# State-space kernel and its parameter gradients: phases from three-piece bf16 matmuls wrapped by an integer mask, inner sums over 128 positions

## The chip, the core and the metric

The kernel runs on one core of one Trainium2 chip. The metric is the device time of one launch in microseconds (us); where several timed runs of a kernel are quoted, it is their median. PE is the matmul engine, VectorE (DVE in the profile), ScalarE (ACT) and GpSimd (POOL) are the other compute engines.

## The reference, cut to what matters

The block is a layernorm, a diagonal state-space convolution, a gated feed-forward network, and the gradients of all of it. The change touches what makes the convolution kernel and its parameter gradients:

```python
# D = 576 channels, N = 128 states, L = 2048 positions
logdA = dt * (A_re + 1j * A_im)
P = jnp.exp(logdA[:, :, None] * l[None, None, :])       # D x N x L
K = jnp.einsum("dn,dnl,dn->dl", Cc, P, dB).real         # the convolution kernel
y = irfft(rfft(pad(xn)) * rfft(pad(K)))[..., :L] + u * Dskip
out = x + y * silu(ffn(xn))
# wanted: out and the gradients of u, A, B, C, log_dt, Dskip, w1, w3, w2
```

The complex exponential is never formed for all L positions. A position is split as an inner and an outer part, l = inner + width x outer; exp, sine and cosine are made for the inner table (Q) and for the outer one (P), and products of the two are summed by matmuls over the states. The gradient of A, B, C and dt needs sums of gK(l) P(l) and of l gK(l) P(l) over all l, and uses the same split.

## The kernel before

It has three parts that matter here. **Kernel generation**: for each chunk of 16 channels, fp32 matmuls against selector matrices (constants with one run of numbers per channel) make phase and decay rate times position; VectorE reduces the phase to a fraction of a turn in two fp32 passes; ScalarE takes sine, absolute value and cosine.

```python
# kernel generation, one chunk (cut)
pt = ps.tile([P, 512], FP32, name="tau_ps")
nc.tensor.matmul(pt[:], lhsT=self.thp[rows, c, :], rhs=SELQ[rows, cols], ...)   # fp32
nc.scalar.copy(out=tauQ[:, j * 512:(j + 1) * 512], in_=pt[:])
pe = ps.tile([P, 512], FP32, name="e_ps")
nc.tensor.matmul(pe[:], lhsT=self.rho[rows, c, :], rhs=SELQ[rows, cols], ...)   # fp32
nc.scalar.activation(out=EQ[:, j * 512:(j + 1) * 512], in_=pe[:], func=ACT.Exp)
...
# gen_trig
nc.vector.tensor_scalar(out=u[:], in0=tau[:], scalar1=MAGIC, scalar2=-MAGIC, op0=ALU.add, op1=ALU.add)
nc.vector.tensor_tensor(out=fr[:], in0=tau[:], in1=u[:], op=ALU.subtract)
nc.scalar.activation(out=S[:], in_=fr[:], func=ACT.Sin, scale=TWO_PI_S)
nc.scalar.activation(out=A[:], in_=fr[:], func=ACT.Abs)
nc.scalar.activation(out=C[:], in_=A[:], func=ACT.Sin, scale=-TWO_PI_S, bias=self.halfpi_col[:])
```

**The correlation gradient gK**: PE's inverse transform, written in halves of 64 positions; ScalarE stores it as `gK2[:, :, jpos]`, bf16 elements 64 bytes apart.

```python
for h in range(2):
    ...
    nc.tensor.matmul(pt[64 * h:64 * (h + 1), 0:DH], lhsT=lw, rhs=rh, ...)     # 64 output rows
nc.scalar.copy(out=gK2[:, :, jpos], in_=pt[:, 0:DH])
```

**The parameter sums**: a loop over 36 pieces; VectorE multiplies rates broadcast to 64 rows by the position, reduces them, forms Q; PE contracts Q with gK over 64 positions; ScalarE copies the result out of PSUM; VectorE makes four long fp32 passes and one reduction.

```python
nc.vector.tensor_tensor(out=prodR[:], in0=Tsb[:], in1=Pzr[:, :, None, :].to_broadcast(...), op=ALU.mult)
nc.vector.tensor_tensor(out=prodI[:], in0=Tsb[:], in1=Pzi[:, :, None, :].to_broadcast(...), op=ALU.mult)
nc.vector.tensor_tensor(out=comb[:, :, 0:2, :], in0=prodR[:, :, 0:2, :], in1=prodI[:, :, 2:4, :], op=ALU.subtract)
nc.vector.tensor_tensor(out=comb[:, :, 2:4, :], in0=prodR[:, :, 2:4, :], in1=prodI[:, :, 0:2, :], op=ALU.add)
nc.vector.reduce_sum(out=red[:]..., in_=comb[:]..., axis=AX.X)
```

## Time and profile before

The kernel before took 3373.16 us (median of three runs, 3367.8 to 3374.43). The page of the profile gives the busy time of each engine over the span, and then the span in 40 slices with the busy share in tenths:

```profile
span 3370.4 us, 46694 instructions
...
PE 2351.0 (70%) x19198; PEld 1532.3 (45%) x19198; DVE 1926.4 (57%) x2713; ACT 1468.8 (44%) x1878; POOL 263.5 (8%) x503
...
PE   1999994845999794836231111129999999965999
PEld 1444442532333572625121111117777777753777
DVE  6677778475444457365889999954334443310222
```

One slice is 84 us. PE is full in slices 2 to 6 (kernel generation), VectorE in slices 22 to 26 (the parameter sums), so the averages of 70% and 57% hide two stages that each have a bound of their own. Each stage ends with its last VectorE work, except the convolution and feed-forward, which are cut where the first matmul of the gK stage starts:

| Stage of the kernel before | us | bound by |
|---|---|---|
| start, layernorm, kernel generation | 552.7 | PE, fp32 matmuls |
| convolution and feed-forward | 732.7 | not touched |
| gK and input gradient | 425.9 | PE and VectorE in turns |
| parameter sums | 486.7 | VectorE |
| final gradients, left behind the loop | 24.9 | VectorE, small instructions |
| feed-forward gradients to the end | 1147.5 | not touched |

These are two lines of VectorE's timeline before (start, length, instruction): passes that build the selectors stand between the layernorm's own short instructions.

```profile
22.74 4.41 DVE L297 SCALAR_TENSOR_TENSOR SELQ<-v 128x4096 f32<-128x4096 f32 x1
27.07 0.16 DVE L143 RECIPROCAL rstd<-sd 128x1 f32<-128x1 f32 x1
...
28.71 4.37 DVE L298 SCALAR_TENSOR_TENSOR SELQ<-v,SELQ 128x4096 f32<-128x4096 f32 x1
```

### The profile page before, as it was taken

The page shows a single profiled execution, that of the slowest core. Times are in us where ns is not written, and L with a number is a line of the kernel's source. Part 1 is how long each engine was busy: PE and PEld are TensorE (multiplying, and loading weights), DVE is VectorE, ACT ScalarE, POOL GpSimd, SP SyncE. Part 2 cuts the span into 40 slices and gives each one's busy share as a digit, 9 for nine tenths or more (in the row PEclk, how much of TensorE's full clock was granted, in tenths as well). Part 3 has the DMA queues.
Part 4 walks back from the last instruction along what each step waited for, and adds up shares of the span by engine and source line. Part 5 has one row for each costly group of instructions (what it writes and reads, how often), then busy time and mean ns, then how long its engine had stood idle before and what let it go on. Part 6 is the DMA issues. An engine that isn't in the chain of part 4 may idle for free.

```text
span 3370.4 us, 46694 instructions
## 1 busy us (share of the span) xinstructions
PE 2351.0 (70%) x19198; PEld 1532.3 (45%) x19198; DVE 1926.4 (57%) x2713; ACT 1468.8 (44%) x1878; POOL 263.5 (8%) x503
## 2 busy tenths in 40 slices
PE   1999994845999794836231111129999999965999
PEld 1444442532333572625121111117777777753777
DVE  6677778475444457365889999954334443310222
ACT  2888886601444113511055666527555555510000
POOL 1000000001111110000000000002222222110000
PEclk8555555977999896967665555559999999987999
DMA  2000000205666762011043333246544444347532
GB/s 79 19 21 21 22 21 13 101 34 183 236 225 218 251 208 97 1 41 51 27 124 97 100 96 96 69 132 172 148 136 140 137 138 137 108 103 203 201 148 82
DMA packets 323880, 373.57 MB, mean 111 GB/s; under 512 B 106577, under 2 KB 274898, under 8 KB 320466
## 3 DMA queue, kind: packets, MB, share of 16 engines
q1 hardware_dynamic: 172226, 132.36, 13.7%
q10 hardware_dynamic: 117888, 129.08, 12.3%
q0 software_dynamic: 33552, 109.15, 9.6%
q8 instruction: 150, 2.46, 0.3%
q14 instruction: 64, 0.52, 0.1%
HBM read 201.84 MB, written 152.14 MB: 105 GB/s over the span
## 4 chain that ended last, share of the span: by engine, by line
PE 40%; DVE 26%; issue 18%; DMA 7%; POOL 3%; SPq 3%; ACT 2%; ACTq 0%; POOLq 0%; DVEq 0%
PE px L1293 8%; PE ph L1200 4%; PE tau_ps L353 4%; PE e_ps L356 4%; PE dft_ps L496 3%; SPq L1105 3%; DVE red L1005 2%; PE gk_ps L857 2%; DVE prodI L997 2%; PE e_ps L365 2%; DMA out_dram<-gw 2%; PE pgw L1241 2%; PE tau_ps L362 2%; PE inv_ps L607 2%; PE pgw L1229 2%
## 5 line engine op out<-in xcount | busy, mean ns | idle before, releaser
L984 PE MATMUL pT<-gK,QTr 64*128 64x32 bf16 x576 | 71.0, 185 | 331.7 <-DVE QTr L970 318.7
L1293 PE MATMUL px<-w1T,ggc 128*128 128x288 bf16 x1152 | 237.8, 289 | 42.1 <-DMA w1T<-in_B_w_dram 42.1
L1293 PE MATMUL px<-w3T,guc 128*128 128x288 bf16 x1152 | 237.6, 289 | 27.5 <-DMA guc<-GU_dram 19.1
L1241 PEld LDWEIGHTS <-xn_bf 128*128 128x128 bf16 x2304 | 226.7, 99 | 58.5 <-issue 29.9
L984 PEld LDWEIGHTS <-QTr 64*128 64x128 bf16 x1152 | 64.5, 101 | 355.0 <-DVE QTr L970 322.5
L691 DVE CAST g_t<-pg 128x1024 bf16<-128x1024 f32 x72 | 88.2, 1224 | 182.3 <-ACT s_t L690 182.3
L1244 DVE CAST gw<-pgw 128x256 bf16<-128x256 f32 x144 | 60.1, 423 | 228.1 <-DMA out_dram<-gw 130.7
L683 PEld LDWEIGHTS <-wmB_w 128*128 128x128 bf16 x1152 | 107.4, 98 | 161.6 <-issue 44.2
L1297 DVE TENSOR_TENSOR gx<-px,gx 128x288 f32<-128x288 f32 x32 | 13.1, 452 | 291.4 <-PE px L1293 291.4
L1200 PE MATMUL ph<-go_oT,w2T 128*128 128x512 bf16 x720 | 169.6, 382 | 0.5 <-ACT gh L1203 0.5
L1310 ACT ACTIVATE t<-gx 128x576 f32<-128x576 f32 x16 | 10.9, 683 | 362.1 <-DVE gx L1297 362.1
L1229 PE MATMUL pgw<-go_o,h_n 128*128 128x288 bf16 x1152 | 165.4, 286 | 0.0
L727 PE MATMUL po<-w2res,hc 128*128 128x288 bf16 x1152 | 146.4, 289 | 17.4 <-DMA hc<-H_dram 17.4
L1241 PE MATMUL pgw<-gg_n,xn_bf 128*128 128x256 bf16 x1152 | 135.0, 279 | 26.7 <-DVE gw L1244 26.7
L690 ACT ACTIVATE s_t<-pg 128x1024 bf16<-128x1024 f32 x72 | 73.8, 1024 | 168.7 <-PE pu L688 168.7
L1293 PEld LDWEIGHTS <-ggc 128*128 128x128 bf16 x1152 | 113.6, 99 | 72.6 <-issue 43.2
L683 PE MATMUL pg<-xnT,wmB_w 128*128 128x512 bf16 x576 | 138.5, 383 | 9.7 <-DMA xnT<-XNT_dram 9.7
L353 PE MATMUL tau_ps<-SELQ,thp 64*128 64x512 f32 x144 | 143.2, 1096 | 0.3 <-ACT WiT L242 0.3
L1293 PEld LDWEIGHTS <-guc 128*128 128x128 bf16 x1152 | 113.5, 99 | 58.4 <-DMA guc<-GU_dram 19.6
L683 PE MATMUL pu<-xnT,wmB_w 128*128 128x512 bf16 x576 | 138.0, 383 | 0.0
L356 PE MATMUL e_ps<-SELQ,rho 64*128 64x512 f32 x144 | 137.5, 1057 | 0.0
L1241 PE MATMUL pgw<-gu_n,xn_bf 128*128 128x256 bf16 x1152 | 137.5, 273 | 0.0
(361 smaller groups left out, 6352.0 us busy)
## 6 DMA issues: line engine op xcount, KB each, us to landing
U_dram<-u_t POOLq DMA_DIRECT2D x36, 512.0 KB, 3.1
G_dram<-g_t POOLq DMA_DIRECT2D x36, 512.0 KB, 4.1
H_dram<-h_t SPq DMA_DIRECT2D x36, 512.0 KB, 5.2
hc<-H_dram SPq DMA_DIRECT2D x8, 2304.0 KB, 10.1
rep_r<-RT_dram SPq DMA_DIRECT2D x72, 256.0 KB, 4.4
rep_t<-RT_dram ACTq DMA_DIRECT2D x72, 256.0 KB, 3.9
gate<-G_dram POOLq DMA_DIRECT2D x36, 512.0 KB, 5.4
up<-U_dram POOLq DMA_DIRECT2D x36, 512.0 KB, 6.3
```

Of the source, the lines that this page charges most:

```text
L353: nc.tensor.matmul(pt[:], lhsT=self.thp[rows, c, :], rhs=SELQ[rows, cols], start=True, stop=True)
L356: nc.tensor.matmul(pe[:], lhsT=self.rho[rows, c, :], rhs=SELQ[rows, cols], start=True, stop=True)
L496: nc.tensor.matmul(pt[:, 0:pw], lhsT=mat[:, tt, kc * P:(kc + 1) * P], rhs=src_fn(tt)[:, po:po + pw], start=(tt == 0), stop=(tt == KT - 1))
L683: nc.tensor.matmul(pt[:, o:o + 512], lhsT=wm[w][:, c, cs], rhs=xnT[:, c, t0:t0 + 512], start=(c == 0), stop=False)
L691: nc.vector.tensor_copy(out=g_t[:, hs], in_=pg[:])
L727: nc.tensor.matmul(po_[:, pi_, 0:pw], lhsT=hc[:, fi, k * P:(k + 1) * P], rhs=self.w2res[:, fi, po:po + pw], start=(fi == 0), stop=(fi == F ...
L984: nc.tensor.matmul(pT[:, gi, kind, :], lhsT=lhs[rows, dl, :], rhs=rhs[rows, dp, :], start=True, stop=True)
L1105: self.nc.sync.dma_start_transpose(out=dst, in_=src)
L1200: nc.tensor.matmul(ph[:, q * 512:(q + 1) * 512], lhsT=w2T[:, c, :], rhs=go_oT[:, c, hh * HL + q * 512:hh * HL + (q + 1) * 512], start=(c = ...
L1229: nc.tensor.matmul(pgw[pi_][:, 0:pw], lhsT=h_ns[fl][:, tt, :], rhs=go_o[:, tt, po:po + pw], start=(tt == 0), stop=(tt == LT - 1))
L1241: nc.tensor.matmul(pw_[:, 0:GW], lhsT=self.xn_bf[:, tt, c * P:(c + 1) * P], rhs=nat[:, tt, :], start=(tt == 0), stop=(tt == LT - 1))
L1293: nc.tensor.matmul(px[pi_][:, 0:pw], lhsT=act[:, fi, k * P:(k + 1) * P], rhs=wT[:, fi, po:po + pw], start=(fi == 0 and ai == 0), stop=(fi ...
```

## The change

The intent: make PE's and VectorE's part of the phases cheap. Each rate is split into three bf16 pieces, whose sum has nearly fp32's precision; a bf16 matmul against bf16 selectors adds them, plus a large constant that puts the fraction of a turn into the low bits of the fp32 result. One integer mask on VectorE then wraps the phase, in place of two fp32 passes and a copy. The sums over positions use 128 inner positions instead of 64, so that gK needs no halves.

The core of the diff, with cuts marked by `...`:

```diff
+    def split_rates(self, tmp):                      # three bf16 pieces of each rate, to DRAM
...
+        for q, src in enumerate((thr, th64, self.rho)):
+            for k in range(3):
+                nc.vector.tensor_copy(out=pc[:, k], in_=r[:])
+                if k < 2:
+                    nc.vector.tensor_tensor(out=r2[:], in0=r[:], in1=pc[:, k], op=ALU.subtract)
...
 # kernel generation
-                    nc.tensor.matmul(pt[:], lhsT=self.thp[rows, c, :], rhs=SELQ[rows, cols], ...)
-                    nc.scalar.copy(out=tauQ[:, j * 512:(j + 1) * 512], in_=pt[:])
+            nc.tensor.matmul(pt[:], lhsT=LT_[:, ch, :], rhs=SEL[:, o:o + 512], ...)         # bf16
+            nc.vector.tensor_scalar(out=m[:, o:o + 512], in0=pt[:].bitcast(I32), scalar1=(1 << 17) - 1,
+                                    scalar2=None, op0=ALU.bitwise_and)
...
+            for g in range(NCH // GE):               # GE = 6: exponentials of six chunks first
...
 # gK
-                                nc.tensor.matmul(pt[64 * h:64 * (h + 1), 0:DH], lhsT=lw, rhs=rh, ...)
-                        nc.scalar.copy(out=gK2[:, :, jpos], in_=pt[:, 0:DH])
+                                nc.tensor.matmul(pt[:, 0:pw], lhsT=lw, rhs=rh, ...)
+                            nc.scalar.copy(out=gK[:, t_tile, po:po + pw], in_=pt[:, 0:pw])
...
 # parameter sums, one chunk of 16 channels
+        S, C = self.trig(gen, m, 16, W_, "q")
+        for (q, src) in ((qi, S), (qr, C)):
+            nc.vector.tensor_tensor(out=q[:]..., in0=E[:], in1=src[:], op=ALU.mult)
+        pz = tp_.tile([P, 3, LT, DC], BF16, name="pz")
+        self.dma(pz[:], self.PZ_dram[:, ch])
+        for dl in range(DC):
+            for k, q in enumerate((qi, qr)):
+                nc.tensor.matmul(pT[:, dl, k, :], lhsT=q[:, dl, :], rhs=gKK[:, :, :, d0 + dl], ...)
+        for s in range(2):
+            for kind in range(2):
+                nc.vector.tensor_tensor(out=pr[:, :, kind], in0=pT[:, :, :, kind * LT:(kind + 1) * LT],
+                                        in1=pz[:, s:s + 2].rearrange("p r a d -> p d r a"), op=ALU.mult)
+            nc.vector.tensor_reduce(out=S_all[...], in_=pr[:]..., op=ALU.add, axis=AX.X)
```

Names that come up again: SBUF is the on-chip memory and PSUM the memory that matmuls write to; a pool is a piece of either that is reserved for tiles, and the built order is the order in which the scheduler has put the instructions on each engine. In the parameter sums, m is the masked phase, E the exponential, S and C the sine and cosine, qi and qr the inner table (E times S and C), pT PE's product of that table with gK, and pz the outer table by which VectorE multiplies pT. One turn of this loop handles a pair of chunks.

## The prediction

> **What bounds the kernel now.** I read the busy table by stretches first, with stretches cut where the line numbers change, then each stretch's groups of instructions with shapes kept apart, then the chain of work that ended last. The three stretches that the change touches:
>
> ```profile
> 85.00:552.00 467.00, 457.74 (x2733) 199.79 (x2732) 337.90 (x539) 379.11 (x505) 0.00 (x0) 0.50 0.06 21
> 1379.00:1556.00 177.00, 96.02 (x896) 81.79 (x897) 100.01 (x75) 45.75 (x32) 0.00 (x0) 0.76 0.09 27
> 1735.00:2198.00 463.00, 75.81 (x2185) 66.64 (x2185) 457.78 (x501) 267.08 (x314) 0.00 (x0) 0.50 0.34 91
> ```
>
> After the stretch's length the columns are PE, weight loads, VectorE, ScalarE, GpSimd, then granted clock, DMA share and GB/s. So kernel generation (467 us) is PE-bound at 98%; the correlation gradient gK (177 us) has nothing saturated; the parameter sums (463 us) are VectorE-bound at 99%, with PE nearly idle. Their groups of instructions:
>
> ```profile
> L353 PE MATMUL tau_ps<-SELQ,thp 64*128 64x512 f32 x142 | 141.1, 1096 | 0.0
> L356 PE MATMUL e_ps<-SELQ,rho 64*128 64x512 f32 x144 | 137.5, 1057 | 0.0
> L277 ACT ACT_TABLE_LOAD x37 | 47.5, 1283 | 0.7
> ...
> L997 DVE TENSOR_TENSOR prodI<-Tsb,Pzi 128x2048 f32<-128x2048 f32 x36 | 82.2, 2283 | 0.0
> L995 DVE TENSOR_TENSOR prodR<-Tsb,Pzr 128x2048 f32<-128x2048 f32 x36 | 82.2, 2283 | 1.6 <-ACT Tsb L986 1.1 <-DMA rep_r<-RT_dram 0.5
> L1005 DVE TENSOR_REDUCE red<-comb 128x64 f32<-128x2048 f32 x36 | 82.0, 2276 | 0.0
> ```
>
> Kernel generation runs 432 fp32 matmuls of about 1.08 us: 467 us, its whole length. The parameter sums spend five sixths of VectorE on fp32 passes. In gK the chain shows that VectorE and PE take turns:
>
> ```profile
> 1405.33 25.91 PE gk_ps L857 x253
> ...
> 1584.22 16.89 PE gu_ps L895 x125
> ```
>
> While PE does 256 half-width matmuls (64 output rows) in 26 us, VectorE waits 24.6 us for the Z buffers, because two Z tiles serve both this block and the next. The second row is the same product written with 128 output rows, in the input gradient: 125 matmuls in 16.9 us, 135 ns each.
>
> **What the Trainium skill says.** (1) "VectorE: DVE Perf Modes", section "The perf-mode tier table": tensor_tensor runs two elements per cycle for bf16 in SBUF, one for fp32 or PSUM; tensor_reduce always one. The trace agrees: bf16 1024 elements 683 ns, 512 elements 425, fp32 1024 elements 1216-1225; and the bf16 product with a factor broadcast along the innermost axis takes 692 ns for 512, the slow rate. (2) "ScalarE: Activation LUTs", section "What ACT_TABLE_LOAD costs": about 1283 ns a load, then a drain of 1380. The trace has 1283, but the next activation starts at once (load at 304.75, exp at 306.04), so I count 1.28 a switch. The page's 93 ns for a column bias fits: 1132 with, 1057 without, at 1024 elements. (3) "TensorE: Matmul & The Clock Gate", section "Back-to-back issue gap": a small matmul has a floor near 25 ns and N/1.2 ns on the throttled clock. The small matmuls here start every 26.5 ns; the granted clock was 0.50. (4) "SBUF — State Buffer", section "Door 1: The DMA port swizzle", has a note that accesses which move to a new 16-byte line every element pay a penalty. The gK evacuation, which writes bf16 64 bytes apart, agrees: 1430 ns for 288 elements, against 588 for 512 contiguous ones in another cast.
>
> **The change, part by part.** Durations are from rows above or scaled from them; starts of successive instructions on ScalarE and VectorE overlap by about 0.09 us in the timeline, which I take off. I also read the order in which the changed program's instructions stand on each engine.
>
> *Kernel generation.* Twelve fp32 matmuls per chunk of 16 channels become six bf16 ones (0.43 us at half clock: 2.6 us). With the 64 small ones (1.85 us in the timeline) PE needs under 5 us of a chunk's former 12.8. VectorE per chunk: three masks from PSUM (0.69 each, one element per cycle), bf16 products 2x0.68, 2x0.43, 2x0.68, 2x0.43, a negation 0.25, the KT copy 0.42: 7.2, or 6.6 with overlaps. ScalarE: three exponentials (0.52), three trigonometric passes of 1536 (1.55, so 1.47 apart): 6.0. The batching by six chunks is meant to save table loads, but in the built order the scheduler scatters it: ten loads per six chunks (52 in the stage, before 73). A group costs ScalarE 18x0.52 + 18x1.47 + 10x1.28 = 49 us and VectorE 40. Walking one group through both orders, VectorE waits some 11 us in the burst of exponentials, and the group closes after about 51.5 us. Six groups: 309, less 12 for the last one without a successor, plus 5 for its end. The start moves: splitting rates costs 12 us of VectorE, then 45 small stores and 9 loads through DRAM, each waiting for an earlier slot; I let the first sine start at 107 instead of 93. The end comes at 107 + 309 - 12 + 5 = 409; I take 415 for 552: **137 us off**.
>
> *gK.* 896 half-width matmuls become 448 of 135 ns. A block with 256 goes from 26 to 17.3, three times, and the first block gets 4.5 back: **31 us off**, on the path because of the turns. The cheaper evacuation (ScalarE was idle) is worth nothing.
>
> *Parameter sums.* Removed: range reduction, four fp32 passes of 1024 to 2048 and ScalarE's 144 copies. Per pair of 16-channel chunks VectorE now has eight masks (0.62), four bf16 products of 2048 (1.2), eight products from PSUM of 512 (0.63) and four sums of 1024 (1.2): 19.6 us, where 25.7 were. ScalarE has eight exponentials, six passes of 2048 (1.9) and four table loads (71 in all, before 50): 21 us. If these overlapped, the loop would take 21x18 = 378 us. But the built order does not let them. From the sine of chunk c: S(c), A(c), S(d), C(c), A(d), load, exp, load, C(d) end at 14.6. VectorE does qi(c) at 2.5, waits for S(d) to 5.8, for C(c) to 7.7, then 2 us for PE's 32 products of c, which need qr(c); its multiply-and-sum ends at 15.9; qr(d), 2 us more for PE, multiply-and-sum of d, and only then the last masks of the next chunk, at 26.7. The next sine waits for these. So VectorE idles 7 us of 26.7, and 18 pairs take 480 us. With the build of gKK (7.5) and a start of 3 the last sum comes 490 us after the convolution ends, before 487.
>
> *The tail.* The new pools are closed before the final gradients, and in the built order all of these stand after the last sum on VectorE; before, most lay within the loop. They are 46 us + 9 for W, with 3 of latency 58, against 25 (2198 to 2223): **33 us on**.
>
> Sum: 3373 - 137 - 31 + 3 + 33 = 3241. I put 3250, since the strided reads below can only add.
>
> **Rivals.** *The parameter loop overlaps fully*: bound by ScalarE's 378 us, 100 us better, about 3140. For it: PE's 32 products might take 0.9 us rather than 2. Against: that alone gives 43 us; the order of masks and sums is fixed. *Strided reads turn costly*: the 32 moving columns now lie 1152 bytes apart, and the factor pz is read 32 bytes apart. If the 144 products take 1.2 instead of 0.69 us, the loop gains 76 us: 3320, within 2%. For it: the 1430 ns of gK. Against: VectorE reads PSUM at 64-byte strides (KT copy, 256 elements in 424 ns) at full rate, though that is not SBUF. *Kernel generation turns VectorE-bound or stalls on PE's order*: 60 us a group would return 50 us: 3300. *A stage hidden anyway* does not fit: each stage is followed by one that waits for it.
>
> **Range and chances.** I give the parameter loop an error of 45 us, kernel generation 20, start and tail together 15; as independent errors their squares add to one of 51. An 8-in-10 range is 1.28 times that on either side, 65, which I shift a little towards the slow side for the strided reads: 3190 to 3320. Two per cent faster means under 3307: 0.84. Within 2%: 0.15. Slower: 0.01.
>
> **What would show it.** In the profile after: the stage of kernel generation 410 to 430 us of end time, with ScalarE the busiest and about 52 loads; masks near 0.69 us; gK's chain blocks near 17 us; VectorE under 80% busy in the parameter loop, waiting for ScalarE's S and C and for PE's pT, with some 26 us per pair; the final gradients in one stretch of about 55 us with ScalarE idle. Wrong if the multiply rows read over 1 us, if pT products start further apart than 60 ns, or if the pair takes 21 us.

## The result, and the profile after

The changed kernel is correct and took **3264.9 us** (median of four runs, 3264.14 to 3271.57), against 3373.8 us for the kernel before in the same rounds (3367.8 to 3375.72). The ratio is 0.9685, 95% interval 0.9667 to 0.9702: faster by a little over 3%. Such a ratio is the mean time of one kernel's runs over that of the other's in the same rounds, so not quite the ratio of the medians.

The page of the profile after:

```profile
span 3262.9 us, 43023 instructions
...
PE 2197.4 (67%) x17602; PEld 1417.2 (43%) x17670; DVE 1750.6 (54%) x2690; ACT 1424.8 (44%) x1626; POOL 256.0 (8%) x504
...
PE   1556556499979854453444444169899999956999
PEld 1232235333337633331111111047677777744777
DVE  6586847734435657678777777734343444310222
```

PE is no longer full in slices 2 to 5, and VectorE's run of nines has become sevens: it now waits in the parameter sums. The busy table by stretches of the changed kernel (kernel generation, gK, parameter sums, final gradients; columns as in the prediction), and after it the two stretches of the kernel before that the prediction did not show in this cut:

```profile
85.00:401.00 316.00, 184.87 (x2519) 90.77 (x2520) 225.37 (x481) 286.10 (x269) 0.00 (x0) 0.51 0.11 26
1225.00:1375.00 150.00, 65.99 (x452) 47.74 (x451) 99.60 (x75) 13.39 (x34) 0.00 (x0) 0.70 0.11 35
1528.50:2069.20 540.70, 233.46 (x1452) 98.45 (x1452) 412.24 (x460) 375.35 (x324) 0.00 (x0) 0.50 0.05 15
2069.20:2108.30 39.10, 2.18 (x8) 1.25 (x8) 38.98 (x236) 1.75 (x3) 0.00 (x0) 0.50 0.10 22
```

```profile
1711.00:2198.00 487.00, 80.01 (x2311) 70.42 (x2311) 480.21 (x518) 279.69 (x329) 0.00 (x0) 0.50 0.36 93
2198.00:2223.00 25.00, 2.80 (x12) 2.05 (x12) 24.82 (x150) 1.75 (x3) 0.00 (x0) 0.57 0.11 24
```

The third line after is the surprise. VectorE's work in the parameter sums fell from 480 to 412 us, and yet the stage grew from 487 to 541. By stages, with the prediction's term beside each:

| Stage | before | after | change | predicted |
|---|---|---|---|---|
| to the end of kernel generation | 552.7 | 400.8 | -151.9 | -137 |
| convolution and feed-forward | 732.7 | 730.5 | -2.2 | 0 |
| gK and input gradient | 425.9 | 397.2 | -28.7 | -31 |
| parameter sums | 486.7 | 540.7 | **+54.0** | +3 |
| final gradients behind the loop | 24.9 | 39.1 | +14.2 | +33 |
| feed-forward gradients | 1147.5 | 1154.6 | +7.1 | 0 |
| span | 3370.4 | 3262.9 | -107.5 | -132 |

In kernel generation the groups of instructions show ScalarE's share: two of its rows, and the mask that took the place of the fp32 passes.

```profile
L398 DVE TENSOR_SCALAR m_k<-t_ps 128x512 int32<-128x512 int32 x108 | 70.7, 682 | 28.2 <-ACT A_k L304 16.6 <-PE t_ps L397 11.6
L382 ACT ACTIVATE E_g<-e_ps 128x512 bf16<-128x512 f32 x108 | 57.3, 620 | 5.0 <-PE e_ps L381 4.7
...
L382 ACT ACT_TABLE_LOAD x26 | 33.4, 1283 | 0.5
```

With two more rows of loads (17 and 10) there are 53 table loads in the stage. In gK the chain of waits answers to the 25.91 us block before: three blocks of full-width matmuls, 16.8 to 17.7 us.

```profile
1252.29 16.76 PE gk_ps L871 x125
...
1298.10 17.73 PE gk_ps L871 x125
...
1356.02 17.54 PE gk_ps L871 x123
```

For the parameter sums, first the row of the product with pz, then VectorE's timeline over one pair of chunks (in square brackets the idle time before an instruction, and who ended it):

```profile
L1000 DVE TENSOR_TENSOR pr_q<-pT,pz 128x512 f32<-128x512 f32 x144 | 146.9, 1061 | 72.0 <-PE pT L996 72.0
```

```profile
1815.67 1.23 DVE L990 TENSOR_TENSOR qi<-E_q,S_q 128x2048 bf16<-128x2048 bf16 x1 [2.33 <-ACT S_q L302]
1817.57 1.23 DVE L990 TENSOR_TENSOR qr<-E_q,C_q 128x2048 bf16<-128x2048 bf16 x1 [0.67 <-ACT C_q L306]
1820.84 3.03 DVE L1000 TENSOR_TENSOR pr_q<-pT,pz 128x512 f32<-128x512 f32 x3 [2.04 <-PE pT L996]
...
1830.41 3.02 DVE L1000 TENSOR_TENSOR pr_q<-pT,pz 128x512 f32<-128x512 f32 x3 [2.05 <-PE pT L996]
...
1837.18 4.26 DVE L984 TENSOR_SCALAR m_q<-q_ps 128x512 int32<-128x512 int32 x7
```

The four waits sum to 7.1 us a pair, as the prediction had walked them. The masks recur at 1807.95 and 1837.18: a pair takes 29.2 us, not 26.7. The row explains the rest: 1061 ns a product, where 0.63 us (0.69 less the overlap) had been counted. A pair has eight of them, so 8 x 0.37 = 3.0 us; in the whole loop 144 x 0.37 = 53 us, close to the 51 by which the stage missed its predicted +3.

### The profile page after: what moved, and what is told of

Read it like the earlier page. It is cut to its first block, busy times and chain, and to the rows that moved or that the text cites. A ratio compares the mean times of both kernels' runs of the same rounds, so it can differ in the third digit from the quotient of the medians.

```text
span 3262.9 us, 43023 instructions
## 1 busy us (share of the span) xinstructions
PE 2197.4 (67%) x17602; PEld 1417.2 (43%) x17670; DVE 1750.6 (54%) x2690; ACT 1424.8 (44%) x1626; POOL 256.0 (8%) x504
## 4 chain that ended last, share of the span: by engine, by line
PE 29%; DVE 21%; issue 18%; ACT 7%; DMA 5%; POOL 3%; SPq 3%; ACTq 0%; POOLq 0%; DVEq 0%
PE px L1283 8%; PE ph L1190 4%; DVE pr_q L1000 3%; PE dft_ps L516 3%; SPq L1095 3%; PE pgw L1231 2%; ACT S_q L302 2%; DMA out_dram<-gw 2%; PE inv_ps L627 2%; PE pT L996 2%; DVE S_all L1002 2%; PE gk_ps L871 2%; PE pgw L1219 2%; PE gu_ps L906 2%; ACT A_q L304 2%
## 5 line engine op out<-in xcount | busy, mean ns | idle before, releaser
L1000 DVE TENSOR_TENSOR pr_q<-pT,pz 128x512 f32<-128x512 f32 x144 | 146.9, 1061 | 72.0 <-PE pT L996 72.0
L996 PE MATMUL pT<-gKK,qr 128*128 128x32 bf16 x576 | 69.7, 233 | 145.8 <-DVE qr L990 145.8
L1190 PE MATMUL ph<-go_oT,w2T 128*128 128x512 bf16 x682 | 161.2, 380 | 1.4 <-ACT gh L1193 0.3
L1283 PEld LDWEIGHTS <-guc 128*128 128x128 bf16 x1152 | 113.3, 98 | 59.1 <-DMA guc<-GU_dram 20.2
L996 PEld LDWEIGHTS <-qr 128*128 128x128 bf16 x576 | 63.9, 122 | 167.6 <-DVE qr L990 167.6
L747 PEld LDWEIGHTS <-hc 128*128 128x128 bf16 x1152 | 112.2, 99 | 48.1 <-issue 18.4
```

Source lines behind the costliest of these rows:

```text
L747: nc.tensor.matmul(po_[:, pi_, 0:pw], lhsT=hc[:, fi, k * P:(k + 1) * P], rhs=self.w2res[:, fi, po:po + pw], start=(fi == 0), stop=(fi == F ...
L996: nc.tensor.matmul(pT[:, dl, k, :], lhsT=q[:, dl, :], rhs=gKK[:, :, :, d0 + dl], start=True, stop=True)
L1000: nc.vector.tensor_tensor(out=pr[:, :, kind], in0=pT[:, :, :, kind * LT:(kind + 1) * LT], in1=pz[:, s:s + 2].rearrange("p r a d -> p d r a ...
L1190: nc.tensor.matmul(ph[:, q * 512:(q + 1) * 512], lhsT=w2T[:, c, :], rhs=go_oT[:, c, hh * HL + q * 512:hh * HL + (q + 1) * 512], start=(c = ...
L1283: nc.tensor.matmul(px[pi_][:, 0:pw], lhsT=act[:, fi, k * P:(k + 1) * P], rhs=wT[:, fi, po:po + pw], start=(fi == 0 and ai == 0), stop=(fi ...
```

## The experiments

The theory to be tested: (a) the slow product comes from reading pz 32 bytes apart, nothing else; (b) the loop is set by a cycle of dependences between VectorE, ScalarE and PE, not by the throughput of ScalarE with its table loads; (c) kernel generation is set by ScalarE after PE was relieved, and some 18 us of its gain are no matter of matmuls but of the selectors that left the layernorm; (d) gK's gain is PE's time alone. Twelve kernels were run. In stages that a run did not touch they differed by some us (convolution and feed-forward took 728.8 to 734.1 us in the fourteen traces, the feed-forward gradients 1154.5 to 1161.6 us in the changed kernel and those made from it). The parameter sums and final gradients together, which most runs aim at, took 579.8 us in the changed kernel.

### 1. The product reads pz contiguously (wrong order on purpose)

```diff
-                                        in1=pz[:, s:s + 2].rearrange("p r a d -> p d r a"), op=ALU.mult)
+                                        in1=pz[:, s:s + 2].rearrange("p r d a -> p d r a"), op=ALU.mult)
```

> The changed kernel with one edit: the 144 products in the parameter loop read the factor pz along its contiguous axis (the two inner axes taken in the other order; both are 16 long, so the result is wrong on purpose for the parameter gradients). Theory: the 32-byte stride of that read is what makes the product 1061 ns instead of 690. Then the product falls to about 690 ns, the cycle of two chunks from 29.2 to about 26.4 us, and the program by 144 x 0.37 = 53 us, to about 3212 (3200 to 3225). Rival: the PSUM operand or the mix of fp32 and bf16 makes it slow; then the product stays at 1061 ns and the time at 3263.

Measured 3214.3 us (single look; parameter gradients wrong, as intended). The row:

```profile
L1000 DVE TENSOR_TENSOR pr_q<-pT,pz 128x512 f32<-128x512 f32 x144 | 92.5, 684 | 71.9 <-PE pT L996 71.9
```

The PSUM operand, the types, the count and the wait for pT are as they were; only the stride of one bf16 operand differs, and 1061 ns became 684. A pair takes 26.1 us. The loop fell from 540.7 to 486.0 us, within 4 us of the 490 that the prediction had for it. Point (a) holds and the rival falls.

### 2. No table loads in the parameter loop (wrong)

```diff
-                        nc.scalar.activation(out=E[:, o:o + 512], in_=pe[:], func=ACT.Exp)
+                        nc.scalar.activation(out=E[:, o:o + 512], in_=pe[:], func=ACT.Abs)
```

> The changed kernel with the exponentials of the parameter loop replaced by absolute values, which need no other table (wrong result on purpose): 71 table loads of 1.28 us fewer on ScalarE, 91 us. Theory: the loop is set by a cycle of dependences between VectorE, ScalarE and PE on which at most one load in a pair lies, so the time falls by 0 to 23 us (3240 to 3263) and VectorE's waits for pT of 2 us stay. Rival: ScalarE with its loads bounds the loop; then some 60 to 91 us go, 3170 to 3200.

Measured 3248.8 us (single look); the loop took 519.0 us. Of 90 us of table loads taken away, 22 came back, at the upper end of what the cycle allows. The waits for S and C did not move (42.0 and 12.0 us in all, 42.4 and 12.0 in the changed kernel); those for pT fell from 72.0 to 52.7:

```profile
L1000 DVE TENSOR_TENSOR pr_q<-pT,pz 128x512 f32<-128x512 f32 x144 | 146.9, 1060 | 52.7 <-PE pT L996 52.7
```

That is 19 of the 22 us, so the expectation that these waits would stay was wrong in part; why PE's products come earlier without the loads was not followed up. The loads are mostly off the path, and point (b) holds against the rival that ScalarE with its loads bounds the loop.

### 3. No table loads in kernel generation (wrong)

The same edit in the other stage.

> The changed kernel with the exponentials of kernel generation replaced by absolute values (wrong result on purpose): 53 table loads fewer, 68 us of ScalarE. Theory: with the fp32 matmuls gone, ScalarE sets this stage (286 of 316 us busy), so most of it is won: 45 to 60 us, to 3203 to 3218, and ScalarE still the busiest at over 85%. Rival: the stage waits in turns on VectorE and PE as the parameter loop does; then under 20 us, 3243 to 3263.

Measured 3228.9 us (single look), between the two ranges. The stage ended at 357.0 instead of 400.8, 44 us for 67 us of loads (52 of the 53 went), just short of the 45 expected; 8 us of it were lost in later stages that the edit did not touch. But ScalarE was not over 85% busy. The window of the stage (columns as above):

```profile
85.00:357.00 272.00, 183.24 (x2519) 92.01 (x2520) 222.63 (x481) 216.22 (x217) 0.00 (x0) 0.50 0.13 31
```

Over these 272 us ScalarE had 216 and VectorE 223. Point (c) is half right: ScalarE is ahead in the changed kernel, and with the loads gone VectorE is level at once, neither of them full.

### 4. gK in halves again

```diff
-                            for idx, (lw, rh) in enumerate(mms):
-                                nc.tensor.matmul(pt[:, 0:pw], lhsT=lw, rhs=rh, ...)
+                            for hf in range(2):
+                                for idx, (lw, rh) in enumerate(mms):
+                                    nc.tensor.matmul(pt[64 * hf:64 * hf + 64, 0:pw], lhsT=lw[:, 64 * hf:64 * hf + 64], rhs=rh, ...)
```

> The changed kernel with only one part undone: the correlation gradient's matmuls are split into two halves of 64 output rows again, 896 instead of 448, same result, same evacuation and layout. Theory: PE's 26 us a block against 17 lie on the path because PE and VectorE take turns there; the stage grows by 26 to 31 us, the time to 3289 to 3294. Rival: the gain came from the cheaper evacuation on ScalarE or from the layout; then the time stays within 8 us of 3263.

Measured 3295.6 us (single look, correct), 2 us above the range. The three blocks of the chain were back at 27.12, 26.38 and 25.29 us and the stage at 424.2 us, 27 longer, although layout and evacuation stayed those of the change. Point (d) holds: for the evacuation (398 ns instead of 1430) and the layout together less than 2 of the 28.7 us are left, which is within the scatter.

### 5. Only the matmuls of kernel generation in bf16, in the kernel before

```diff
-        SELQ = selp.tile([P, KS * BV], FP32, name="SELQ")
+        SELQ = selp.tile([P, KS * BV], BF16, name="SELQ")
...
-                    nc.tensor.matmul(pt[:], lhsT=self.thp[rows, c, :], rhs=SELQ[rows, cols], ...)
+                    nc.tensor.matmul(pt[:], lhsT=thb[rows, c, :], rhs=SELQ[rows, cols], ...)
```

> The kernel BEFORE with one part of the change alone: selectors, theta and rho are stored as bf16, so that its 432 matmuls of kernel generation become single-pass bf16; everything else stays (fp32 passes, copies, table loads; too coarse a phase, so wrong on purpose). PE falls from 458 us to about 260. Theory: the stage is then set by ScalarE (379 us busy) and VectorE (338), so it ends near 465 to 480 instead of 552 and the time is 3285 to 3305: about 80 of the 152 us come from the matmuls alone, the rest from the lighter trigonometry and from the earlier start. Rival: the fp32 matmuls were the whole matter; then 3220 to 3240.

Measured 3316.4 us (single look). The stage ended at 496.7, so 56 us off, less than the 80 expected. The windows of that run:

```profile
82.00:497.00 415.00, 181.37 (x2520) 95.88 (x2519) 328.82 (x547) 371.27 (x504) 0.00 (x0) 0.50 0.07 24
```

PE fell to 181 us, not to the 260 expected, because the count of 432 matmuls was wrong. The kernel issues six fp32 matmuls a chunk, 216 in the stage; each leaves two records in the trace, which start 0.854 us apart. In this run there are 216 records, and where they follow one another directly they start 0.427 us apart: an fp32 matmul of 512 columns took four times as long as a bf16 one at the same granted clock of 0.50. ScalarE with its copies, six short trigonometric passes a chunk and 71 loads was busy for 371 of 415. So PE's relief alone meets the next bound after 56 of the 152 us. The change also made ScalarE's passes longer and fewer, saved loads and lightened VectorE; what each of these gave was not tested one by one.

### 6. The kernel before without the building of its selectors (wrong)

The body of the selector building became two memsets on GpSimd.

> The kernel BEFORE, with the building of its selectors replaced by two memsets on GpSimd (wrong on purpose). Theory: those VectorE passes of about 20 us stood within the layernorm and held everything after it; without them all later work starts 15 to 20 us earlier: 3354 to 3360. Rival: they lay in VectorE's free time there; then the time stays at 3370 to 3376.

Measured 3351.3 us (single look). The layernorm's last VectorE work came at 35.4 us instead of 52.2, and kernel generation ended at 535.9 instead of 552.7: 16.8 us, the expected 15 to 20. The time fell by a few us more, to below the expected range, because stages that were not touched ran shorter in this run (scatter as named above). The changed kernel's layernorm ends at 34.5. Its selectors take 7.2 us of VectorE instead of 20.2, in shorter passes, and only 4.7 us of that lie within the layernorm. So about 17 of its 152 us come from there: run 6 shows it for the kernel before, and the changed kernel's layernorm ended earlier by as much. With the 56 of run 5 that leaves some 79 us for ScalarE's and VectorE's lighter work, less what the splitting of the rates costs, if the parts add up, which was not tested.

### 7. pz made contiguous by GpSimd

```diff
         self.dma(pz[:], self.PZ_dram[:, ch])
+        pzt = tp_.tile([P, 3, DC, LT], BF16, name="pzt")
+        nc.gpsimd.tensor_copy(out=pzt[:], in_=pz[:].rearrange("p r a d -> p r d a"))
...
-                                        in1=pz[:, s:s + 2].rearrange("p r a d -> p d r a"), op=ALU.mult)
+                                        in1=pzt[:, s:s + 2].rearrange("p r d a -> p d r a"), op=ALU.mult)
```

> The changed kernel with a right result: GpSimd, idle otherwise, copies pz into the order in which VectorE reads it contiguously, one copy of 768 elements per chunk. Theory: the product reads 690 ns again and the time is that of the run with the wrong order, 3212 to 3220. Rival: GpSimd's copies slow VectorE down or arrive late; then 3225 to 3270.

Measured 3224.9 us (single look, correct), a miss by 5 us and at the lower edge of the rival's range: the rival came true in small. Parameter sums and final gradients took 533.9 us, 46 less than in the changed kernel and 9 more than in the first experiment. One group shows where 6 of the 9 went: the mean of the product qr rose from 1220 to 1397 ns (36 of them); the waits for pT grew by 3 us. The timelines of GpSimd and VectorE in this run:

```profile
1806.95 1.56 POOL L994 COPY pzt<-pz 128x768 bf16<-128x768 bf16 x1 [16.65 <-DVE pr_q L1002]
...
1808.00 1.59 DVE L990 TENSOR_TENSOR qr<-E_q,C_q 128x2048 bf16<-128x2048 bf16 x1
```

The second qr of a pair starts while GpSimd's copy runs, and lasts 1.59 us instead of 1.22. The Trainium skill, "SBUF — State Buffer", section "Who interferes with whom", says that a VectorE instruction with two SBUF inputs contends with a GpSimd instruction that reads SBUF, and that the second to issue blocks until the first has finished. The trace agrees: the copy ends at 1808.51, 0.5 us after qr's start (GpSimd's ends are rough in a profile), and 0.37 us were lost. A pair takes 26.7 us in this run (qr at 1799.88 and 1826.58), against 26.1 in run 1; that this is the prediction's figure is chance, as the prediction had no copy on GpSimd.

### 8. and 9. Pools open over the final gradients, and the one edit this needed

To keep the loop's pools open, room was made by writing the absolute value over the mask:

```diff
-        A = sb.tile([P, n_el], FP32, name="A_" + tagp)
+        A = m[:].bitcast(FP32)
...
-            self.param_sums(gK, S_all)
-            self.phase5_final(fin, S_all, ps2)
+            self.param_sums(gK, S_all, fin, ps2)     # calls phase5_final before its pools close
```

> The run before it with the pools of the loop kept open over the final gradients (room for it comes from writing the absolute value over the mask), so that four of the five blocks of final gradients stand within the loop in the built order, as in the kernel before. Theory: the tail falls from 39 to about 10 us, but VectorE has to do the four blocks in the loop all the same; what its waits there (about 7 us of a pair) take up is won: 5 to 25 us against the run before it, so 3190 to 3212. Rival: the blocks lengthen the cycle by all that they take: no change.

Measured 3171.7 us (single look, correct; the tail fell to 7.8 us), 53 us less than run 7, more than twice what was expected at most. The edit had done two things at once: the built order of the loop was another one, with 36 table loads instead of 70. So the shared tile was run alone:

> The changed kernel with GpSimd's contiguous pz and with the absolute value written over the mask, but with the pools closed before the final gradients as in the changed kernel: the one edit that the run with the open pools had beside them, alone. In the built order it takes the table loads of the parameter loop from 70 to 36 and puts both chunks' multiply-and-sum side by side, behind both qr. If the order alone shortened the pair from 26.7 to 25.3 us, the loop takes 18 x 1.4 = 25 us less than with GpSimd's copy alone and the time is 3195 to 3205, with the tail still 39 us; the open pools are then worth the 25 to 33 us that are left of the 53. If the order is worth nothing, 3220 to 3228.

Measured 3204.9 us (single look, correct): the loop took 470.0 us against 494.8 in run 7, so 25 us came from the order and, by the tail and the rest (481.1 against 509.1 us for sums and final gradients together), 28 from the open pools. The row of the product in run 7, and the rows of the product and of qr in run 9, show what the order did:

```profile
L1002 DVE TENSOR_TENSOR pr_q<-pT,pzt 128x512 f32<-128x512 f32 x144 | 92.5, 684 | 74.5 <-PE pT L998 74.5
```

```profile
L1007 DVE TENSOR_TENSOR pr_q<-pT,pzt 128x512 f32<-128x512 f32 x144 | 92.2, 682 | 3.8 <-PE pT L1003 3.8
L995 DVE TENSOR_TENSOR qr<-E_q,C_q 128x2048 bf16<-128x2048 bf16 x36 | 44.1, 1226 | 92.1 <-ACT C_q L991 92.1
```

The waits for pT are gone, as PE's products of one chunk now lie beside VectorE's work on the other. But most of this waiting moved: VectorE now waits 92.1 us for the cosine, where it waited 12.0 in run 7, and 16.7 for the sine instead of 42.4. In all it waits 16 us less; another 8 us came from VectorE's work, 6 of them because qr is no longer slowed by GpSimd's copy (1226 ns instead of 1397). So "the order" is three things at once here, with the 34 table loads that it saves (44 us of ScalarE), and what each gave alone was not tested. That a smaller buffer gives a faster loop is a matter of the scheduler's order, not of the chip.

### 10. The loop one pair behind

```diff
+                new = [self.param_exp(g * GE + j, rts, SELB, ep, ps0) for j in range(GE)]
+                ms = [self.param_mask(it, rts, SELB, gen, ps0) for it in new]
+                trs = [self.param_trig(m, gen) for m in ms]
+                for it in pend:                       # products and sums of the pair before
+                    self.param_back(it, S_all, tp_)
+                pend = [self.param_q(it, tr, gKK, gen, tp_, ps) for it, tr in zip(new, trs)]
```

> As the run with open pools, with the loop written one pair of chunks behind: masks and trigonometry of pair g+1 are issued before the products and sums of pair g, so that VectorE has work while ScalarE and PE prepare. Theory (a dependency cycle, not an engine's throughput, sets the loop): the pair falls from 25.3 to about 21 us, VectorE over 90% busy in the loop, the time to 3085 to 3125. The final gradients fall behind the loop again in the built order (about 30 us of tail), as VectorE has no gaps left for them. Rival: the loop is at an engine's limit already, or PE's products stand in the way again: 3150 to 3175.

Measured **3128.7 us** (median of four, 3124.09 to 3131.69, correct; ratio to before 0.9274, 95% interval 0.9261 to 0.9288), 4 us outside the expected range. Its timeline and windows:

```profile
1770.78 1.23 DVE L1018 TENSOR_TENSOR qr<-E_q,C_q 128x2048 bf16<-128x2048 bf16 x1 [0.21 <-ACT C_q L1005]
1772.69 1.89 DVE L1038 TENSOR_TENSOR pr_q<-pT,pzt 128x512 f32<-128x512 f32 x3 [0.69 <-PE pT L1026]
...
1777.20 4.87 DVE L993 TENSOR_SCALAR m_q<-q_ps 128x512 int32<-128x512 int32 x8 [0.90 <-PE q_ps L992]
...
1791.71 1.23 DVE L1018 TENSOR_TENSOR qr<-E_q,C_q 128x2048 bf16<-128x2048 bf16 x1 [0.21 <-ACT C_q L1005]
```

```profile
1531.30:1930.60 399.30, 225.83 (x1452) 99.14 (x1452) 361.50 (x476) 328.83 (x290) 73.11 (x36) 0.50 0.08 21
```

The pair takes 20.9 us (1770.78 to 1791.71), as worked out, and 1.8 us of it are waits. The loop is 399 us for 541, with 361.5 us of VectorE's work in it: 91% busy. VectorE had as much work as in run 9 (361.5 us, before 355.8), ScalarE too (328.8, before 329.9, with 36 loads in both), and PE hardly less (225.8, before 231.4); the order alone took 470 to 399 us. That is the strongest evidence for point (b). As expected, 33 us of final gradients fell behind the loop again.

### 11. and 12. Exponentials of kernel generation batched for real

On top of run 10: groups of nine chunks, one buffer of exponentials, the absolute value over the mask; then also four mask buffers.

```diff
-        GE = 6
+        GE = 9
...
-                self.tc.tile_pool(name="kg_e", bufs=2) as ep, \
+                self.tc.tile_pool(name="kg_e", bufs=1) as ep, \
...
-        m = sb.tile([P, TW], I32, name="m_k")
+        m = sb.tile([P, TW], I32, name="m_k", bufs=4)      # run 12 alone
```

> The run before it, with kernel generation's exponentials batched for real: groups of nine chunks, one buffer for the exponentials, the absolute value written over the mask; 11 table loads in the stage instead of 53. Theory: the run without any load there showed 35 us for 68 us of loads; 42 loads fewer are 54 us of ScalarE, and the single buffer puts the exponentials of a group where VectorE has little to do, so 15 to 35 us are won: 3060 to 3100. Rival: the single buffer costs what the loads gave: no change against the run before it.

Measured 3134.9 us (median of four, 3133.57 to 3138.55; ratio 0.9297): a miss. The loads fell from 53 to 9 and ScalarE's work in the stage by 53 us, yet the stage ended at 408.6 instead of 401.4. Two of its waits (total, times, longest):

```profile
ACT S_k L401 <- DVE m_k L398: 79.7, 18, 11.2
DVE q_k L409 <- ACT C_k L405: 69.2, 20, 14.2
```

ScalarE now waited 79.7 us for masks, and VectorE 69.2 us for cosines. The time is the rival's; that the single buffer is the cause is not shown. Of the other edits, the shared tile keeps a mask's buffer taken until the cosine has been read, and run 12 looks at that.

> As the run with exponentials batched by nine, with four mask buffers instead of two. In that run ScalarE waited 80 us for masks and VectorE 69 us for the cosines, both about 238 us busy of 323. Theory: with two mask buffers VectorE can't run ahead while ScalarE does a group's 27 exponentials; with four it does, ScalarE's wait falls under 45 us and the stage ends 20 to 40 us earlier: 3095 to 3115. Rival: VectorE's order (products of a chunk behind later masks) keeps the wait: 3125 to 3137.

Measured **3116.4 us** (median of four, 3114.94 to 3120.05; ratio 0.9238, 95% interval 0.9223 to 0.9254), the best of the versions. The stage ended at 394.4, 14 us before run 11's, less than the 20 to 40 expected, so that the time just missed its range; ScalarE's wait for masks fell to 48.8 us, not under 45. Only the number of mask buffers differs from run 11, so these 14 us had hung on it and not on the single buffer of exponentials. Both engines are still under 77% busy (235 and 223 us of 309), so this stage, too, is set by the hand-over between them, and what a better order would give was not tried.

## Why the prediction was right

The time was put at 3250 with a range of 3190 to 3320 and came at 3265. Its sum was 3241, and in the traces 24 us separate the fall of 132 from the 107.5 measured; but this is a sum of errors of opposite sign: 51 us too hopeful in the parameter sums, 7 in the feed-forward gradients and 2 in gK, against 19 us in the tail, 15 in kernel generation and 2 in the convolution the other way. That the number came so close is luck in that part; the mechanisms below are what was right. Of the signs that it named, five came: about 52 loads (53), masks near 0.69 us (682 ns), gK's blocks near 17 us, VectorE under 80% busy in the loop (76%), waits for S, C and pT. Three did not: kernel generation ended before 410, a pair took 29 us for 26, the tail 39 for 55. And one of its three signs of being wrong came true: the multiply rows read over 1 us. (The products pT started 57 ns apart, under its limit of 60.)

- **Kernel generation** was right in mechanism and in size but for its start. From the first sine to the end the walk had 107 to 415; the trace has 96.7 to 400.8, so 308 predicted and 304 measured; 53 loads where 52 were counted, masks of 682 ns where 0.69 us was. The term that was off is the start: it was put 14 us later than before, for the splitting of the rates. It came 3.5 us later than before only, since the old selectors had held up the layernorm by 17 us (run 6). VectorE's timeline of the layernorm would have shown it; the prediction read that timeline from 58 us on. One reading was wrong without harm: the 432 matmuls of 1.08 us are records, two for each of six fp32 matmuls a chunk. They overlap, as they start 0.854 us apart; together they cover 392 us and not the whole 467, and the small matmuls fill the rest, so that PE was full all the same. And the 93 ns said to fit are 75 in the two numbers given for 1024 elements, and 108 at 512 (721 less 613); nothing in the sum hung on them.
- **gK** was right: blocks of 17 us, 28.7 us for 31 off, and run 4 brings 27 of them back. The cheaper evacuation being worth nothing was right as well.
- **Parameter sums**: the step that failed is one term of the walk, the eight products of a pair at 0.63 us. They took 1061 ns each, and run 1 shows that the stride of pz is the cause. The waits of 2.1, 0.7 and twice 2 us were measured as 2.33, 0.67, 2.04 and 2.05, and with the contiguous operand the loop takes 486 us for the predicted 490. The prediction had this as a rival at 1.2 us and 76 us (144 x 0.51 is 73); it came at 53 us. Against it had been said that VectorE reads PSUM at 64-byte strides at full rate. True, and no argument for SBUF, as the text itself noted: the evidence that did concern SBUF, the 1430 ns evacuation, pointed the right way and got too little weight.
- **The tail** was right in mechanism (all final gradients behind the last sum, ScalarE idle) and too large: 39 us for 58, so +14 instead of +33. The 46 us were a sum of busy times; the trace has 236 instructions in 39.1 us, about 0.27 us long and 0.20 us apart, so that durations of small instructions add up to more than the time they take. For long ones the prediction had taken this overlap off, for these not.
- **The rival of a fully overlapped loop** (about 3140) was rightly set aside for the kernel as built. Run 10 shows that it was a statement on the order alone: with the order changed the loop reaches 399 us.
- **Open**: the feed-forward gradients at the end, the same code, took 7 us more after the change, and 8 to 14 us more in the other kernels made from the changed one, but not in the two made from the kernel before (1146.5 and 1147.1 against 1147.5 us). In the changed kernel PE waited 35 us for weight-gradient buffers there, before 27. The cause was not tested.

## What to carry to other kernels

Walk a loop in its built order, engine by engine, before trusting busy shares: in the changed parameter loop no engine was over 76% busy, 90 us of table loads were worth 22, and a change of order alone took 470 us to 399. Look at the innermost stride of every operand in SBUF, the small factor too, before counting an instruction at its usual rate. When a wait is gone, look for where it went: in run 9, 71 us fewer for pT came with 80 us more for the cosine. And look at what the removed code held up elsewhere: the old selectors cost the layernorm, not their own stage, 17 us.

## What the Trainium skill lacked or had wrong

- "SBUF — State Buffer", section "Door 1: The DMA port swizzle", says that accesses to a new 16-byte line each pay a penalty, without its size. Here it was 377 ns for 512 bf16 elements read 32 bytes apart by a VectorE product (1061 against 684 ns, run 1), 0.74 ns an element. ScalarE's evacuation of gK took 1430 ns for 288 bf16 elements written 64 bytes apart, and 398 ns for as many written contiguously in the changed kernel.
- "VectorE: DVE Perf Modes", section "Mode 1× (REGULAR) — the baseline", lists odd strides among what works in the baseline mode, for which it gives one result a cycle, and names no cost of them. The same instruction was 55% slower with the strided operand than with the contiguous one (1061 over 684 ns).
- "ScalarE: Activation LUTs", section "What ACT_TABLE_LOAD costs", adds a drain of about 1380 ns to each load of 1283 ns. No trace here shows it: in run 10 a load at 1770.76 of 1.28 us is followed by the exponential at 1772.06, and after 176 of the 197 loads of the changed kernel ScalarE's next instruction starts within 1.4 us of the load's start.
- No page that was read tells how far the order that a scheduler builds can decide: 36 or 70 table loads, and 25 us, from sharing one buffer (runs 7 and 9).
